# Front of a retention + squared-ReLU kernel: first pair taken before the second, loads and casts reordered, late loads of q in halves

## The chip, the core and the metric

One core of a Trainium2 chip runs the whole program. The metric is the device time of one execution in microseconds (us). A profiled execution gives the trace that all readings come from. Engines: PE (TensorE), DVE (VectorE), ACT (ScalarE), POOL (GpSimd) and SP, whose queue issues most of the DMAs.

## What is computed

```python
for t in range(S):                      # B=4, H=8, S=768, D=64
    state = gamma * state + k[t] outer v[t]
    y[t] = scale * q[t] @ state
x = y.transpose(0, 2, 1, 3).reshape(3072, 512)
out = relu(x @ w_in) ** 2 @ w_out       # w_in 512 x 2048, w_out 2048 x 512
```

All inputs and the output are float32 in HBM. The recurrence over tokens is done in chunks of 128 tokens: inside a chunk by masked scores (q times k, times v), between chunks by a state.

## The kernel before

There are 24 chunks of 128 tokens (6 for each batch) and 11 blocks of tokens for the feed-forward part: the first has four chunks, the others two each. For each chunk the kernel scales q and k by powers of gamma, turns them (PE transposes at first, DMA transposes from chunk 8 on), multiplies scores, masks them on DVE, updates the state in PSUM (`c_ps`), copies it out in bf16 (`s_bd`), forms the outputs (`y`) and copies them as `xt`, the right side of the feed-forward products. The first product of a block is `xt` times `w_in`, copied out by ACT with ReLU (line 859) and squared on DVE (line 830). The second product with `w_out` is done for most blocks by a seven-product scheme: sums of blocks (`s1` to `s4`) are made on DVE and seven instead of eight products are run on PE (`seven_products`, lines 864 to 984, and for half of the first block `last_of_first`, lines 986 to 1109).

The order of work on each engine is written out by hand: instructions stand on their engine in the order in which the Python program makes them, and each waits on semaphores for what it needs. From line 1289 on, `put(place, what)` hangs a step of later chunks on a numbered place between pieces of feed-forward work.

The front, lines 188 to 198 and 1223 to 1285, prepares the first four chunks in two pairs. **Pair 0** is chunks 0 and 1, **pair 2** is chunks 2 and 3. The steps, as the text below names them (m is the pair, g a group of four heads, j the chunk in the pair):

- `scale_q4`, `transpose_q4`: q of the four chunks. `scale_pair_k(m, g)` (line 588) scales k on DVE, or on POOL if told; `transpose_pair_k(m, g)` (lines 613, 614): four transposes on PE, then a copy `kT` on ACT.
- `scores_pair(m, g)` (line 629): 16 small matmuls on quarter tiles of the array, and two masks for DVE (line 637), called `mask_a` and `mask_b`.
- `cast_pair_v(m, r)` (lines 598, 600): v to bf16, on POOL or ACT.
- `state_pair(m, j)` (lines 656, 667, 669): eight matmuls into `c_ps`, then two copies to `s_bd`.
- `outputs_pair(m, g)` (line 680): 16 small matmuls. `finish_pair(m, j)` (lines 696, 708, 710): four matmuls with the state (none for j = 0 of pair 0), then one copy to `xt` on ACT or DVE.
- `first_pair(n)` (line 1128): eight matmuls of the feed-forward part on pair 0 (L850), then ReLU. It needs `xt` of pair 0 and half of the first quarter of `w_in` in bf16. `first_unit(0, 0, c)` (line 1113): 16 matmuls for chunk c of pair 2, c = 2 or 3.
- `cast_w("in", g, halves, on)` (line 348): w_in to bf16 in eight pieces; the letters name the engine of each piece (V DVE, S ACT, G POOL).
- `keep_awake(n)` (line 371): matmuls on zeros between the steps.

After `first_unit(0, 0, 3)` and `state_pair(2, 1)` comes the **dense stage**: 48 matmuls of 512 columns (L850), from 20.32 us on, and then PE work without end until the last block.

The loads of the front go out on SP in this order: q of heads 0 to 3, half of k of pair 0, q of heads 4 to 7, the other half of k of pair 0, k of pair 2, v of pair 0, v of pair 2, then the four quarters of `w_in`, the first two of them in halves. Loads of w_out go out on POOL's queue. `load_q(m, heads)` (line 88) loads q of chunks m and m+1, in as many DMAs as there are parts in `heads`; chunks 6, 8 and 10 have two parts (`heads_of`), chunks 4 and 12 to 22 have one.

Of the kernel before, what the change touches and what calls it, by code (L numbers as in the profile page):

```python
# [14 lines left out]
ALU = mybir.AluOpType  # L15
# [16 lines left out]
def kernel(  # L32
# [9 lines left out]
    nc = tc.nc  # L42
    P = nc.NUM_PARTITIONS

    B, H, S, D = q.shape
# [40 lines left out]
    raw_q, raw_k, raw_v = {}, {}, {}  # L86
# [23 lines left out]
    def load_pair(m, name, src, to, heads=slice(0, H)):  # L110
        b, i = chunks[m]
        if m not in to:
            t = ldpool.tile([P, 2 * H * D], FP32, name=name)
            to[m] = t.rearrange("s (h r d) -> s r h d", h=H, r=2)
        src = src[b, heads, i * C : (i + 2) * C, :].rearrange("h (s r) d -> s h r d", r=2)
        nc.sync.dma_start(to[m].rearrange("s r h d -> s h r d")[:, heads], src)
# [72 lines left out]
    load_pair(0, "kn", k, raw_k, heads_of[0])  # L189
    load_q4(1)  # L190
    load_pair(0, "kn", k, raw_k, heads_of[1])
    load_pair(2, "kn", k, raw_k)
    load_pair(0, "vn", v, raw_v)
    load_pair(2, "vn", v, raw_v)
    load_w_in(0, parts=2)
    load_w_in(1, parts=2)
    for g in range(2, NQ):
        load_w_in(g)
# [180 lines left out]
    def end_awake():  # L379
        idle_ps.clear()  # L380
# [92 lines left out]
    c_ps = [None]  # L473
# [390 lines left out]
    def seven_products(tb):  # L864
# [17 lines left out]
        def add(out, in0, in1, op=ALU.add):  # L882
            nc.vector.tensor_tensor(out=out, in0=in0, in1=in1, op=op)  # L883
# [16 lines left out]
        def rest():  # L900
            first_sums(slice(4, 8))
            pa = (ps_f if tb == 1 else ps_tp).tile([P, HN], FP32, name="psf" if tb == 1 else "tp")
            pb, pe, pd = (ps_f.tile([P, HN], FP32, name="psf") for _ in range(3))
            oa, ob = (opool.tile([P, DM], FP32, name="osb") for _ in range(2))
            a, u, v = (upool.tile([P, HN], FP32, name=f"u{i}") for i in range(3))
            r0 = first[tb] * C
            for js, stop in ((range(0, 6), False), (range(6, 8), True)):
                product(pa[:], a11, b11, js, True, stop)
                product(pe[:], a22, t4, js, True, stop)
                if stop:  # L910
                    nc.scalar.activation(a[:], pa[:], AF.Copy)
                yield
            add(s3, a11, a21, ALU.subtract)
            product(pd[:], s1, t1, range(8), True, True)
            yield
            add(s4, a12, s2, ALU.subtract)
            product(pb[:], s2, t2, range(8), True, True)
            add(u[:], pb[:], a[:])
            yield
            for js in (range(0, 4), range(4, 8)):  # L920
                product(pa[:], a12, b21, js, False, js[-1] == 7)
                if js[0]:
                    nc.scalar.activation(oa[:, 0:HN], pa[:], AF.Copy)  # L923
                yield
            for js in (range(0, 4), range(4, 8)):
                product(pb[:], s3, t3, js, False, js[-1] == 7)
                if js[0]:
                    add(v[:], pb[:], a[:])
                    add(ob[:, HN:DM], pd[:], v[:])
                    add(ob[:, 0:HN], pe[:], v[:])  # L930

                    def last_product():
                        product(pd[:], s4, b22, range(8), False, True)
                        add(oa[:, HN:DM], pd[:], u[:])
                        yield
                        nc.sync.dma_start(out[r0 + C : r0 + 2 * C], ob[:])
                        yield
                        nc.sync.dma_start(out[r0 : r0 + C], oa[:])
                        yield

                    kept.append(last_product())
                yield
# [43 lines left out]
    def last_of_first():  # L986
# [44 lines left out]
        def second_products():  # L1031
            ops = [ps_f.tile([P, DM], FP32, name="psf") for _ in range(2)]
            pa, pe, pd, pb = (
                t[:, n * HN : (n + 1) * HN]
                for t in [ps_f.tile([P, DM], FP32, name="psf") for _ in range(2)]
                for n in range(2)
            )
            oa, ob = (opool.tile([P, DM], FP32, name="osb") for _ in range(2))
            a, u, v = (upool.tile([P, HN], FP32, name=f"u{i}") for i in range(3))
            r0 = 2 * C  # L1040

            def plain(j):
                for f in (2 * j, 2 * j + 1):
                    for c, op in enumerate(ops):
                        nc.tensor.matmul(  # L1045
                            op[:],
                            lhsT=h_of(0, f)[:, 0, c * C : (c + 1) * C],
                            rhs=w_out_bf[f // FPQ][:, f % FPQ, :],
                            start=(f == 0),
                            stop=(f == NFB - 1),  # L1050
                        )
                product(pa, a11, b(0, 0), (j,))

            lo, hi = range(0, 4), range(4, 8)
            for j in range(4):
                plain(j)
                yield
            product(pd, s1, t1, lo)
            product(pb, s2, t2, lo, False)
            yield  # L1060
            for j in range(4, 6):
                plain(j)
                yield
            product(pe, a22, t4, lo, False)
            yield
            plain(6)
            yield
            plain(7)
            nc.scalar.activation(a[:], pa, AF.Copy)

            def store(c):
                osb = opool.tile([P, DM], FP32, name="osb")
                nc.scalar.activation(osb[:], ops[c][:], AF.Copy)
                nc.sync.dma_start(out[c * C : (c + 1) * C], osb[:])

            store(0)
            yield
            product(pd, s1, t1, hi)
            product(pb, s2, t2, hi)
            add(u[:], pb, a[:])  # L1080
            yield
            store(1)
            product(pa, a12, b(1, 0), lo, False)
            yield
            product(pa, a12, b(1, 0), hi, False)
            nc.scalar.activation(oa[:, 0:HN], pa, AF.Copy)
            yield
            product(pb, s3, t3, lo, False)
            yield
            product(pb, s3, t3, hi, False)  # L1090
            add(v[:], pb, a[:])
            add(ob[:, HN:DM], pd, v[:])
            yield
            product(pe, a22, t4, hi)
            add(ob[:, 0:HN], pe, v[:])

            def last_product():
                product(pd, s4, b(1, 1), range(8), False)
                add(oa[:, HN:DM], pd, u[:])
                yield  # L1100
                nc.sync.dma_start(out[r0 + C : r0 + 2 * C], ob[:])
                yield
                nc.sync.dma_start(out[r0 : r0 + C], oa[:])
                yield

            kept.append(last_product())
            yield
# [130 lines left out]
    keep_awake(1)  # L1238
    transpose_pair_k(0, 1, *f)
    mask_a(0)  # L1240
    scale_pair_k(2, 0)
    mask_a(1)
    scale_pair_k(2, 1, nc.gpsimd)
    keep_awake(1)
    transpose_pair_k(2, 0, ps_c, "c_ps")
    mask_b = scores_pair(0, 1, (tp, f), small_pt())
    mask_b(0)
    mask_b(1)
    keep_awake(1)
    cast_pair_v(0, 0)  # L1250
    cast_pair_v(0, 1, on_scalar=True)
    transpose_pair_k(2, 1, *f)
    cast_pair_v(2, 0)
    cast_pair_v(2, 1)
    mask_a = scores_pair(2, 0, (st, f), spare[:, 0:1024])
    keep_awake(1)
    end_awake()
    mask_a(0)
    mask_a(1)
    state_pair(0, 0)  # L1260
    outputs_pair(0, 0, ((ps_y, "y"), f))
    outputs_pair(0, 1)
    mask_b = scores_pair(2, 1, (tp, f), spare[:, 1024:2048])
    mask_b(0)
    cast_w("in", 0, (0,), "GG-V")
    mask_b(1)
    finish_pair(0, 0)
    finish_pair(0, 1)
    cast_w("in", 0, (0,), "--S-")
    state_pair(0, 1, "SV")  # L1270
    outputs_pair(2, 0, ((ps_y, "y"), st))
    first_pair(0)
    cast_w("in", 0, (1,), "GGVV")
    outputs_pair(2, 1)
    finish_pair(2, 0)
    state_pair(2, 0, "VV")
    first_pair(1)
    finish_pair(2, 1, on_scalar=False)
    cast_w("in", 1, (0,), "VVGG")
    first_unit(0, 0, 2)  # L1280
# [10 lines left out]
    parts = {}  # L1291

    def put(place, what, *args):
        parts.setdefault(place, []).append((what, args))
# [66 lines left out]
    for m, d in zip(range(PACK_FROM, NCHUNK), done):  # L1361
        attend2(m, d, done[m - PACK_FROM - 1] if m > PACK_FROM else 0,
                *ahead.get(m, (d - 19, d - 16, d - 13, d - 9)))
        if m >= 12 and m % 2 == 0:
            put(d - 29, load_q, m)
    places = {
        (8, "k"): [26 + j // 2 for j in range(8)],
        (8, "v"): [35 + j // 2 for j in range(8)],
# [52 lines left out]
```

## Time and profile before

| what | us |
|---|---|
| median of 3 runs | 202.81 (202.81 to 202.84) |
| the profiled execution, its own time | 202.86 |
| its span, first to last instruction | 201.1 |
| PE busy in it | 194.7 |
| DVE, ACT, POOL busy | 151.0, 128.0, 81.9 |

The span is what the trace shows; 1.8 us of the execution lie around it. A row of the timeline gives start, duration, engine, source line, operation, tiles, count, and in brackets how long the engine sat idle before it and what ended that. Matmuls of one row are pipelined, so a step's price on PE is read from its start to the start of the next row.

### The profile page before, as it was taken

What the parts mean: (1) busy time and instruction counts of PE and PEld (TensorE: products, weight loads), DVE (VectorE), ACT (ScalarE), POOL (GpSimd) and SP (SyncE); (2) the same over time, 40 slices, a digit from 0 to 9 for tenths busy, and PEclk for the clock granted to TensorE, in tenths of its full rate; (3) what the DMA queues carried; (4) which work ended last, traced back from release to release, by engine and by line L of the source; (5) the groups of instructions that cost most, each with busy time, mean ns of one, the idle gap of its engine ahead of it and who ended that gap; (6) DMA issues with size and microseconds to landing.
All of it is one profiled execution on the core that took longest, in us unless ns stands there. A gap on an engine that the chain in (4) does not pass through costs nothing.

```text
span 201.1 us, 5856 instructions
## 1 busy us (share of the span) xinstructions
PE 194.7 (97%) x2361; PEld 164.6 (82%) x2361; DVE 151.0 (75%) x327; ACT 128.0 (64%) x260; POOL 81.9 (41%) x154
## 2 busy tenths in 40 slices
PE   7799999999999999999999999999999999999992
PEld 2478445779988999899999999999999999999881
DVE  3987899799698896687697697697696696484472
ACT  8885875264853676774766866864865865845710
POOL 8664760899930762154522185116362202200000
PEclk9999999999999999999999999999999999999999
DMA  5999999999988999598998399989899552101102
GB/s 168 355 375 397 345 191 193 231 229 224 313 176 190 169 229 177 165 138 177 186 181 188 115 169 231 210 195 132 148 175 182 173 93 65 71 0 51 56 0 106
DMA packets 92299, 36.03 MB, mean 179 GB/s; under 512 B 68592, under 2 KB 88304, under 8 KB 92272
## 3 DMA queue, kind: packets, MB, share of 16 engines
q1 hardware_dynamic: 73136, 31.47, 65.1%
q0 software_dynamic: 19136, 4.20, 23.0%
q8 instruction: 18, 0.29, 0.6%
q14 instruction: 9, 0.07, 0.1%
HBM read 27.26 MB, written 6.29 MB: 167 GB/s over the span
## 4 chain that ended last, share of the span: by engine, by line
PE 91%; DVE 3%; DMA 2%; ACT 1%; issue 1%; DVEq 0%
PE psf L850 42%; PE psf L887 21%; PE tp L887 7%; PE psf L1045 3%; PE psf L1011 2%; DMA qn<-in_q_dram 2%; PE st L751 2%; PE y L807 2%; PE y L800 2%; PE c_ps L778 2%; PE c_ps L656 1%; PE y L535 1%; PE st L459 1%; DVE qs L562 1%; PE y L371 1%
## 5 line engine op out<-in xcount | busy, mean ns | idle before, releaser
L850 PE MATMUL psf<-xt,w_in_bf 128*128 128x256 bf16 (+2 forms) x864 | 92.3, 261 | 0.0
L850 PEld LDWEIGHTS <-w_in_bf 128*128 128x128 bf16 x864 | 70.7, 98 | 11.2
L859 ACT ACTIVATE h<-psf 128x512 bf16<-128x512 f32 x96 | 56.3, 595 | 23.5 <-PE psf L850 21.2
L729 POOL COPY v_bd<-v 64x512 bf16<-64x512 bf16 x32 | 21.7, 677 | 76.2 <-DVE v L721 75.3
L830 DVE TENSOR_TENSOR h<-h 128x512 bf16<-128x512 bf16 x80 | 33.0, 428 | 18.5 <-ACT h L859 18.1
L887 PEld LDWEIGHTS <-h 128*128 128x128 bf16 x344 | 31.7, 98 | 3.7 <-issue 0.2
L157 POOL DMA_DIRECT2D k_big<-in_k_dram x40 | 26.6, 686 | 0.0
L887 PE MATMUL psf<-w_sum,h 128*128 128x256 bf16 x168 | 23.5, 273 | 0.0
L887 PE MATMUL tp<-w_out_bf,h 128*128 128x256 bf16 x136 | 19.1, 273 | 0.0
L887 PE MATMUL psf<-w_sum,k_bd 128*128 128x256 bf16 x144 | 17.9, 273 | 0.0
L883 DVE TENSOR_TENSOR u<-psf,u 128x256 f32<-128x256 f32 x20 | 8.5, 424 | 12.3 <-PE psf L887 11.4
L883 DVE TENSOR_TENSOR osb<-psf,u 128x256 f32<-128x256 f32 x29 | 11.5, 421 | 6.6 <-PE psf L887 6.3
L887 PEld LDWEIGHTS <-k_bd 128*128 128x128 bf16 x144 | 13.8, 98 | 1.5
L787 ACT ACTIVATE s_bd<-c_ps 64x256 bf16<-64x256 f32 x29 | 10.7, 369 | 6.3 <-PE c_ps L778 6.3
L390 DVE TENSOR_TENSOR qs<-qn,qf 128x512 bf16<-128x512 f32 x20 | 13.7, 690 | 0.0
L788 ACT ACTIVATE s_bd<-c_ps 64x256 bf16<-64x256 f32 x29 | 11.0, 379 | 0.4
L721 DVE TENSOR_TENSOR v<-stage,kf 128x512 bf16<-128x512 f32 x16 | 10.9, 684 | 0.3 <-issue 0.3
L758 DVE TENSOR_TENSOR pt<-st,cmask 128x512 bf16<-128x512 f32 x16 | 11.0, 688 | 0.2
L923 ACT ACTIVATE osb<-tp 128x256 f32<-128x256 f32 x8 | 3.1, 384 | 12.2 <-PE tp L887 12.2
L814 ACT ACTIVATE xt<-y 128x512 bf16<-128x512 f32 x16 | 9.6, 598 | 1.8 <-PE y L807 1.2
L828 ACT ACTIVATE h<-h 128x512 bf16<-128x512 bf16 x16 | 10.1, 629 | 0.5
L883 DVE TENSOR_TENSOR k_bd<-h 128x512 bf16<-128x512 bf16 x18 | 9.9, 552 | 0.3
(148 smaller groups left out, 290.0 us busy)
## 6 DMA issues: line engine op xcount, KB each, us to landing
out_dram<-osb SPq DMA_DIRECT2D x23, 256.0 KB, 2.5
qn<-in_q_dram SPq DMA_DIRECT2D x9, 512.0 KB, 5.4
stage<-in_v_dram SPq DMA_DIRECT2D x32, 96.0 KB, 4.0
stage<-in_moe_w_in_dram SPq DMA_DIRECT2D x4, 512.0 KB, 6.8
stage<-in_moe_w_in_dram SPq DMA_DIRECT2D x2, 1024.0 KB, 10.7
w_out_bf<-in_moe_w_out_dram POOLq DMA_DIRECT2D x4, 512.0 KB, 10.2
kn<-in_k_dram SPq DMA_DIRECT2D x6, 256.0 KB, 5.7
qn<-in_q_dram SPq DMA_DIRECT2D x6, 256.0 KB, 5.8
```

Source lines behind the costliest of these rows:

```text
L157: nc.gpsimd.dma_start(t[rows, 2 * at_w : 2 * (at_w + size), p, hh, :], half_rows(k, b, 2 * p + hh, i + w, size),)
L390: engine.tensor_tensor(out=out, in0=by, in1=table[:, :, None].to_broadcast([P, H, D]), op=ALU.mult)
L721: nc.vector.tensor_tensor(out=v2.rearrange("s (u p) d -> s u p d", u=2), in0=vn, in1=kf2[:, i, :, :, None].to_broadcast([P, 2, NPAIR, D]), ...
L729: nc.gpsimd.tensor_copy(v_bd[rows, :, hh, :], v2[rows])
L758: nc.vector.tensor_tensor(out=pt[:], in0=st[:], in1=cmask2.rearrange("s r t -> s (r t)")[:, None, :].to_broadcast([P, 2 * NPAIR, C // 2]), ...
L787: nc.scalar.activation(s_bd[halves[0], :, 0, :], c[halves[0]], AF.Copy)
L788: nc.scalar.activation(s_bd[halves[1], :, 1, :], c[halves[1]], AF.Copy)
L830: nc.vector.tensor_mul(hv, hv, hv)
L850: nc.tensor.matmul(hp, lhsT=w_in_bf[g][:, cb, fq * 128 : (fq + 1) * 128], rhs=xts[tb][:, cb, cols], start=(cb == 0), stop=(cb == NCB - 1),)
L859: nc.scalar.activation(hv, hp[:], AF.Relu)
L883: nc.vector.tensor_tensor(out=out, in0=in0, in1=in1, op=op)
L887: nc.tensor.matmul(to, lhsT=left[:, j], rhs=right(j) if callable(right) else right[:, j], start=(start and j == 0), stop=(stop and j == NF ...
```

## The change

Four places change.

1. Loads: v of pair 0 goes ahead of k of pair 2, and the first half of w_in's first quarter ahead of v of pair 2.
2. The front's steps: pair 0 is carried through to its outputs before pair 2's k is turned. The casts of w_in's first quarter are spread in another way over POOL, DVE and ACT, the state copies of pair 0 and pair 2 go from DVE to ACT, and the `xt` copy of chunk 0 from ACT to DVE. There is one keep-awake matmul more.
3. In `seven_products` the DVE step that makes `s4` comes one piece later, behind `u`. In `second_products` the copy and store of the second plain output (`store(1)`) come behind the copy of `pa`.
4. `load_q` of chunks 12 to 20 is issued in two halves.

```diff
     load_q4(1)
     load_pair(0, "kn", k, raw_k, heads_of[1])
+    load_pair(0, "vn", v, raw_v)
     load_pair(2, "kn", k, raw_k)
-    load_pair(0, "vn", v, raw_v)
-    load_pair(2, "vn", v, raw_v)
-    load_w_in(0, parts=2)
+    load_w_in(0, parts=2, between=lambda: load_pair(2, "vn", v, raw_v))
     load_w_in(1, parts=2)
...
             product(pd[:], s1, t1, range(8), True, True)
             yield
-            add(s4, a12, s2, ALU.subtract)
             product(pb[:], s2, t2, range(8), True, True)
             add(u[:], pb[:], a[:])
             yield
+            add(s4, a12, s2, ALU.subtract)
...
-            store(1)
             product(pa, a12, b(1, 0), lo, False)
             yield
             product(pa, a12, b(1, 0), hi, False)
             nc.scalar.activation(oa[:, 0:HN], pa, AF.Copy)
+            store(1)
             yield
...
     mask_a(0)
-    scale_pair_k(2, 0)
     mask_a(1)
-    scale_pair_k(2, 1, nc.gpsimd)
-    keep_awake(1)
-    transpose_pair_k(2, 0, ps_c, "c_ps")
+    keep_awake(2)
+    cast_pair_v(0, 0)
+    cast_pair_v(0, 1, on_scalar=True)
     mask_b = scores_pair(0, 1, (tp, f), small_pt())
     mask_b(0)
     mask_b(1)
-    keep_awake(1)
-    cast_pair_v(0, 0)
-    cast_pair_v(0, 1, on_scalar=True)
-    transpose_pair_k(2, 1, *f)
-    cast_pair_v(2, 0)
-    cast_pair_v(2, 1)
-    mask_a = scores_pair(2, 0, (st, f), spare[:, 0:1024])
+    scale_pair_k(2, 1, nc.gpsimd)
+    scale_pair_k(2, 0)
     keep_awake(1)
     end_awake()
-    mask_a(0)
-    mask_a(1)
     state_pair(0, 0)
     outputs_pair(0, 0, ((ps_y, "y"), f))
     outputs_pair(0, 1)
+    finish_pair(0, 0, on_scalar=False)
+    finish_pair(0, 1)
+    transpose_pair_k(2, 0, *f)
+    transpose_pair_k(2, 1, *f)
+    state_pair(0, 1)
+    keep_awake(1)
+    mask_a = scores_pair(2, 0, (st, f), spare[:, 0:1024])
+    end_awake()
+    cast_w("in", 0, (0,), "GGVG")
+    mask_a(0)
+    mask_a(1)
+    first_pair(0)
     mask_b = scores_pair(2, 1, (tp, f), spare[:, 1024:2048])
     mask_b(0)
-    cast_w("in", 0, (0,), "GG-V")
+    cast_pair_v(2, 0)
+    cast_pair_v(2, 1)
+    cast_w("in", 0, (1,), "GGVS")
     mask_b(1)
-    finish_pair(0, 0)
-    finish_pair(0, 1)
-    cast_w("in", 0, (0,), "--S-")
-    state_pair(0, 1, "SV")
+    state_pair(2, 0)
     outputs_pair(2, 0, ((ps_y, "y"), st))
-    first_pair(0)
-    cast_w("in", 0, (1,), "GGVV")
+    first_pair(1)
     outputs_pair(2, 1)
     finish_pair(2, 0)
-    state_pair(2, 0, "VV")
-    first_pair(1)
     finish_pair(2, 1, on_scalar=False)
     cast_w("in", 1, (0,), "VVGG")
     first_unit(0, 0, 2)
...
         if m >= 12 and m % 2 == 0:
-            put(d - 29, load_q, m)
+            put(d - 29, load_q, m, heads_of if m < 22 else (slice(0, H),))
```

## Prediction

> **What bounds the kernel now.** I read the page first, then the busy time by stretches, then the engines' timelines of the first 21 us.
>
> ```profile
> span 201.1 us, 5856 instructions
> PE 194.7 (97%) x2361; PEld 164.6 (82%) x2361; DVE 151.0 (75%) x327; ACT 128.0 (64%) x260; POOL 81.9 (41%) x154
> 100.00:140.00 40.00, 40.00 (x500) 36.38 (x499) 30.24 (x63) 27.03 (x58) 14.47 (x22) 1.00 1.00 179
> ```
>
> PE is busy for 97% of the span, and in the stretch from 100 to 140 us for 40.00 of 40.00, at a granted clock of 1.00. So this kernel is PE's queue of matmuls from end to end: an edit pays only if PE waits less, and it costs what PE waits more. After the start of the dense stage I find two places worth a tenth or more where PE waits (below). All else is the front: when does the dense stage start? Here is PE before that.
>
> ```profile
> 10.46 0.39 PE L371 MATMUL y<-h 128*128 128x512 bf16 x1
> 10.68 0.39 PE L613 MATMUL psf<-ident,k_big 128*128 128x128 bf16 x4
> 11.01 0.24 PE L629 MATMUL st<-qT,kT 64*64 64x128 bf16 x2
> ...
> 11.36 0.39 PE L371 MATMUL y<-h 128*128 128x512 bf16 x1
> 11.68 0.62 PE L656 MATMUL c_ps<-v_bd,k_big 64*128 64x128 bf16 x8
> 12.23 0.24 PE L680 MATMUL y<-pt,v_bd 64*64 64x128 bf16 x1
> ...
> 12.70 0.22 PE L629 MATMUL tp<-qT,kT 64*64 64x128 bf16 x1
> ...
> 13.16 0.40 PE L696 MATMUL psf<-qT,s_bd 128*128 128x128 bf16 x4
> 13.49 0.62 PE L656 MATMUL c_ps<-v_bd,k_big 64*128 64x128 bf16 x8
> ...
> 14.38 1.05 PE L850 MATMUL psf<-xt,w_in_bf 128*128 128x256 bf16 x8
> 15.36 0.24 PE L680 MATMUL y<-h,v_bd 64*64 64x128 bf16 x1
> ...
> 15.71 0.40 PE L696 MATMUL y<-qT,s_bd 128*128 128x128 bf16 x4
> ...
> 17.61 0.40 PE L696 MATMUL st<-qT,s_bd 128*128 128x128 bf16 x4
> 17.84 2.00 PE L850 MATMUL psf<-xt,w_in_bf 128*128 128x128 bf16 x32
> 19.77 0.62 PE L656 MATMUL c_ps<-v_bd,k_big 64*128 64x128 bf16 x8
> 20.32 10.53 PE L850 MATMUL psf<-xt,w_in_bf 128*128 128x512 bf16 x48
> ```
>
> From start to start these rows give the prices: a keep-awake 0.22 (10.46 to 10.68), or 0.32 when other tile shapes follow (11.36 to 11.68); four transposes 0.33; scores 0.35 (11.01 to 11.36); a state 0.55; the outputs of two groups 0.47, of one group 0.35 (15.36 to 15.71); a finish 0.33 (13.16 to 13.49), or some 0.22 before matmuls of its own shape (17.61 to 17.84; transposes alike); a `first_pair` 0.98; both `first_unit` 1.93. There is hardly a gap: the dense stage starts at 20.32 because that much work lies in front.
>
> **The change, part by part.**
>
> *The front.* Up to the keep-awake at 10.46 both programs have the same chain (q, k of pair 0, scores), except that before turns four k tiles of pair 2 at 9.78, in a time in which PE waited anyway. After must do these behind 10.46: +0.22. Summed with the prices above, in the new order, and with no wait at all: keep-awake 0.32, state 0.55, outputs (0,0) 0.24 and (0,1) 0.35, finish 0.22, transposes 0.22 and 0.33, state 0.55, keep-awake 0.32, scores 0.35, `first_pair` 0.98, scores 0.35, state 0.55, outputs 0.35, `first_pair` 0.98, outputs 0.35, two finishes 0.44, units 1.93, state 0.55: 9.93, so the dense stage could start at 20.39. Nothing is saved on PE; the reorder can only add waits. For those I need the other engines.
>
> ```profile
> 10.56 0.69 DVE L637 TENSOR_TENSOR pt<-tp,maskp 128x512 bf16<-128x512 f32 x1 [0.23 <-PE psf L629]
> 11.17 0.68 DVE L637 TENSOR_TENSOR pt<-psf,maskp 128x512 bf16<-128x512 f32 x1
> ```
> ```profile
> 9.43 0.60 ACT L614 ACTIVATE kT<-psf 128x512 bf16<-128x512 bf16 x1 [0.23 <-PE psf L613]
> 10.84 0.63 ACT L598 ACTIVATE v_bd<-vn 128x512 bf16<-128x512 f32 x1
> 12.33 0.77 ACT L667 ACTIVATE s_bd<-c_ps 64x256 bf16<-64x256 f32 x2 [0.38 <-PE c_ps L656]
> 16.14 0.60 ACT L708 ACTIVATE xt<-y 128x512 bf16<-128x512 f32 x1
> ```
> ```profile
> 7.68 2.94 POOL L588 TENSOR_TENSOR k_big<-kn,kfp 128x512 bf16<-128x512 f32 x2 [1.51 <-DMA kn<-in_k_dram]
> 10.57 0.61 POOL L600 CAST v_bd<-vn 128x512 bf16<-128x512 f32 x1
> 12.04 1.18 POOL L600 CAST v_bd<-vn 128x512 bf16<-128x512 f32 x2 [0.86 <-DMA vn<-in_v_dram]
> 13.46 0.82 POOL L358 CAST w_in_bf<-stage 128x256 bf16<-128x256 f32 x2 [0.24 <-DMA stage<-in_moe_w_in_dram]
> 14.81 0.75 POOL L358 CAST w_in_bf<-stage 128x256 bf16<-128x256 f32 x2 [0.53 <-DMA stage<-in_moe_w_in_dram]
> ```
>
> The loads swap slots of one size (512 KB each), so I let each slot keep its landing: v of pair 0 takes the fifth slot, in by about 9.1 (estimate: one slot, some 1.5 us by 10.57 to 12.04, ahead of the sixth), k of pair 2 the sixth, 10.5, w_in's first half 12.0, v of pair 2 13.4, the second half 14.8. Then, step by step:
>
> - v of pair 0 is cast by 9.7 on POOL and, behind `kT` (9.43 + 0.60), by 10.6 on ACT. State (0,0) starts at 10.78, outputs (0,0) at 11.33, (0,1) at 11.57. But (0,1) needs `mask_b(1)`, and that ends as before, at 11.17 + 0.68 = 11.85, since scores (0,1) still hang on the same `kT`. **First wait: 0.34**, to 11.91.
> - Finish (0,1) needs `s_bd`: state ends 11.40, ACT's pair takes 0.77, 12.2. k of pair 2 is ready on DVE at 12.46 (behind the masks) and on POOL near 12.1. Small waits, 0.08 in all. Transposes at 12.52 and 12.74, state (0,1) 13.07, keep-awake 13.62, scores (2,0) 13.94 (ACT's `kT` 13.8), `first_pair(0)` 14.29. Its w_in pieces are cast by 13.3, its `xt` by 13.3: no wait. Scores (2,1) 15.27, state (2,0) 15.62 (v cast by 14.7), outputs (2,0) 16.17, `first_pair(1)` 16.52 (DVE's piece is cast at 16.60 and asked for at 16.74: close), outputs (2,1) 17.50.
> - Finish (2,0) starts at 17.85, finish (2,1) at 18.07, and PE is through at 18.29. The next thing in its queue is `first_unit(0, 0, 2)`, which reads `xt` of (2,0). Before, that copy had time: finish at 15.71, copy 16.14 to 16.74, unit at 17.84, with a state, a `first_pair` and the other finish between. Now only 0.22 us of PE work lies between. The copy starts 0.43 after the finish and takes 0.60, and PE follows some 0.06 later (`s_bd` ends 13.10, PE 13.16): 18.95. **Second wait: 0.66.** The copy of (2,1) on DVE, begun near 18.5, lies beside the first unit.
>
> Dense stage: 20.39 + 0.34 + 0.08 + 0.66 = 21.47, with rounding 21.4 to 21.5: **+1.1 us**. Behind it everything has more time than before: w_in's later quarters land at the old times, and all casts, masks and stores move along. The cover of this sum is that PE is full; no later idle time gives it back.
>
> *`store(1)` and `s4`.* Both stand where PE waits now:
>
> ```profile
> 44.53 1.31 PE L1011 MATMUL psf<-w_sum,h 128*128 128x256 bf16 x8
> ...
> 61.09 1.05 PE L887 MATMUL psf<-w_out_bf,h 128*128 128x256 bf16 x8
> 62.16 0.60 PE L887 MATMUL psf<-w_sum,h 128*128 128x256 bf16 x4
> ```
> ```profile
> 44.32 0.60 ACT L1073 ACTIVATE osb<-psf 128x512 f32<-128x512 f32 x1
> 44.82 0.38 ACT L1086 ACTIVATE osb<-psf 128x256 f32<-128x256 f32 x1
> ```
> ```profile
> 61.09 0.69 DVE L883 TENSOR_TENSOR h<-h,h 128x1024 bf16<-128x1024 bf16 x1
> 61.69 0.42 DVE L883 TENSOR_TENSOR u<-psf,u 128x256 f32<-128x256 f32 x1
> ...
> 108.73 0.43 DVE L883 TENSOR_TENSOR u<-psf,u 128x256 f32<-128x256 f32 x1 [1.12 <-PE psf L887]
> ```
>
> Eight matmuls take 1.31 at 44.53 and 1.05 at 61.09: 0.26 of wait, for the copy of `pa` that ends at 45.20 behind `store(1)`. With the copy first it ends near 44.7 and the wait goes; the next scores then wait some 0.08 for their mask. I take −0.2 (bounds 0 and −0.28). At 62.16 four matmuls stand behind `u`, which stood behind `s4` (61.09): eight matmuls of 0.109 from 61.09 would let them start at 61.96, so −0.18 (bounds 0 and −0.20). In the later blocks DVE idles 1.12 us before `v` (108.73), and `s4`, 0.69, fits there: nothing.
>
> *q in halves.* Five more issues on SP. The list of waits has one line for q:
>
> ```profile
> DVE qs L562 <- DMA qn<-in_q_dram: 1.8, 1, 1.8
> ```
> ```profile
> 57.83 1.17 SPq L94 DMA_DIRECT2D qn<-in_q_dram  x2
> ```
>
> That is the first load of all; no later q was waited for, so an earlier q gains nothing. A half takes SP 0.6 to issue (57.83, two in 1.17), which can push back what stands behind it: stores, loads of v and the DMA transposes of k. I take 0, since no turned k is named in that list either; bounds 0 and +0.6.
>
> *Two rules of the skill.* The Trainium skill, "TensorEngine Tiling (Array Packing)", Key Properties, says that a change of the tiling mode drains the engine. The trace agrees: 0.10 between a keep-awake before its own shape and before another. By that rule alone the order matters for its number of changes, and I count 15 behind 10.46 in the new order against 14: +0.1, which the prices hold already. The Trainium skill, "DMA: Bandwidth & Descriptors", Anatomy of one DMA, (SWDGE path), gives each DMA a fixed 2.0 us, which speaks against halving loads; by it five more would be 10 us of DMA latency, beside PE's work as long as no q is waited for. It is stated for GpSimd's path, and no row here parts latency from transfer.
>
> **The sum**: +1.1 − 0.2 − 0.18 = +0.7. On the profiled execution's 202.86 (span 201.1 and 1.8 around it; 0.05 over the median of 202.81) that is 203.5 us.
>
> **The rivals.**
>
> - *Not slower: the two waits don't come.* Place: the mask at 11.85 and the `xt` copy at 18.3. If both results lay ready when PE asks, only the floor of 20.39 is left, +0.07, and the regained 0.38 wins: 202.86 − 0.31 = 202.55. It decides from where the waits sum to under 0.3. For it: the floor is as low as now. Against: both waits are distances between two instructions that the order fixes, priced by rows. If half of them comes, it is 203.1, no difference. Chance 0.24 for this side: 0.07 faster, 0.17 the same.
> - *The other engines' queues are later than I place them.* DVE's cast for `first_pair(1)` has 0.14 of room, ACT's `kT` for scores (2,0) 0.14, and POOL has one more cast ahead of v of pair 2; POOL's k takes 1.3 to 1.6 (2.94 for two). Half a us late in that row of copies is PE waiting: dense stage near 22, 204.1. Chance 0.15.
> - *The regained waits don't come, or q in halves pushes a turned k behind its scores*: 203.9. Chance 0.08.
> - My forecast, 203.5 give or take 0.3: 0.53.
>
> **Range and chances.** 202.8 to 204.2 leaves out the fast end of the first rival and the far end of the second. 0.2%, 0.4 us, is about what a measurement of this kernel can tell from no change: faster 0.07, same 0.17, slower 0.76.
>
> **What would show it.** In the changed kernel's PE timeline: outputs (0,1) broken off near 11.6 and going on near 11.9; an idle time of about 0.66 ahead of the 32 matmuls of L849, ended by ACT's `xt` copy; the 48 matmuls starting near 21.4; eight matmuls in 1.05 where 1.31 stood; no gap at the u of the second block. I am wrong if the 48 matmuls start before 20.7, or if PE gaps show after them that are not there now.

## The result and the profile after

| what | before | after |
|---|---|---|
| median, us (14 runs each, taken together) | 202.82 (202.80 to 203.11) | 203.28 (203.17 to 203.84) |
| span of the profiled execution | 201.09 | 201.52 |
| landing of the last output | 199.44 | 200.60 |

The ratio of the medians is 1.0022, with a 95% interval of [1.0014, 1.003]: 0.46 us slower, where 0.7 was forecast. The page of after is as full of PE as that of before:

```profile
span 201.5 us, 5862 instructions
PE 195.3 (97%) x2359; PEld 165.0 (82%) x2362; DVE 150.5 (75%) x324; ACT 128.5 (64%) x262; POOL 82.0 (41%) x155
```

So I read PE's timeline, and for each matmul how much later it starts than the same matmul before. First the front (after's lines are one below those of before).

```profile
10.75 0.62 PE L655 MATMUL c_ps<-v_bd,k_big 64*128 64x128 bf16 x8
11.30 0.24 PE L679 MATMUL y<-pt,v_bd 64*64 64x128 bf16 x1
...
11.55 0.22 PE L679 MATMUL psf<-pt,v_bd 64*64 64x128 bf16 x1
11.88 0.21 PE L679 MATMUL y<-pt,v_bd 64*64 64x128 bf16 x1
...
12.24 0.40 PE L695 MATMUL psf<-qT,s_bd 128*128 128x128 bf16 x4
12.48 0.62 PE L612 MATMUL psf<-ident,k_big 128*128 128x128 bf16 x8
...
18.03 0.39 PE L695 MATMUL st<-qT,s_bd 128*128 128x128 bf16 x4
18.88 1.95 PE L849 MATMUL psf<-xt,w_in_bf 128*128 128x128 bf16 x32 [0.46 <-ACT xt L707]
20.76 0.62 PE L655 MATMUL c_ps<-v_bd,k_big 64*128 64x128 bf16 x8
21.31 10.53 PE L849 MATMUL psf<-xt,w_in_bf 128*128 128x512 bf16 x47
```

The dense stage starts at 21.31, 0.99 later than the 20.32 of before. Two waits make it: 11.55 to 11.88 (0.33, of which 0.05 is the pace of these matmuls: 0.28), and 18.03 to 18.88 (0.85, of which the finish itself is 0.22: 0.63). The row of the units names ACT's `xt` copy. What is left, 21.31 − 0.28 − 0.63 = 20.40, is the floor of 20.39 (the prediction's sum without any wait), so next to nothing of the small waits came. The two results came when the prediction had them, the second mask (begun at 11.14) at 11.82 and the copy at 18.83; DVE's and ACT's timelines:

```profile
11.14 0.68 DVE L636 TENSOR_TENSOR pt<-psf,maskp 128x512 bf16<-128x512 f32 x1
```
```profile
18.23 0.60 ACT L707 ACTIVATE xt<-y 128x512 bf16<-128x512 f32 x1
```

Behind the front, the transposes of q in PE's timeline of before, then PE's timeline of after:

```profile
46.80 0.61 PE L420 MATMUL tp<-ident,qs 128*128 128x128 bf16 x8
```
```profile
45.52 1.04 PE L1010 MATMUL psf<-w_sum,h 128*128 128x256 bf16 x8
...
47.59 0.90 PE L419 MATMUL tp<-ident,qs 128*128 128x128 bf16 x8
...
62.18 1.05 PE L886 MATMUL psf<-w_out_bf,h 128*128 128x256 bf16 x8
63.07 0.60 PE L886 MATMUL psf<-w_sum,h 128*128 128x256 bf16 x4
```

Eight matmuls take 1.04 where 1.31 stood, and from the eight to the four behind `u` it is 0.89 instead of 1.07: both old waits are gone. But the eight transposes of q, 0.61 before, take 0.90: a new wait of 0.28, ahead of the fifth. Two more waits stand at the four matmuls that update the state in the later blocks (`state2`, L777): 0.10 and 0.14 ahead of the last of the four, at 94.8 and 139.6, and a little ahead of the ones before it. The shift of PE runs: +0.99 (front), −0.28 (45 us), +0.09 (a mask, 46), +0.29 (transposes of q, 48), −0.18 (62), +0.11 and +0.16 (`state2`) = +1.18. Yet the span is only 0.43 longer. So 0.75 came back **behind the last matmul**.

There SP waits for everything that is still under way. Its DMAs go in turn to eight completion semaphores, here called lanes 0 to 7, and at the end SP waits for lane 0, 1, ... 7 in this order, then drains. SP's instructions of that last line, before and after, from the landing of the last output (199.44 and 200.60) on:

```profile
L1416 SPq EVENT_SEMAPHORE  x6: 28/28/28, 199.5 to 200.2; - x6
L1416 SPq DRAIN  x1: 13/13/13, 200.2 to 200.2; - x1
```
```profile
L1415 SPq DRAIN  x2: 7/10/13, 200.7 to 200.8; - x2
L1415 SPq EVENT_SEMAPHORE  x1: 28/28/28, 200.6 to 200.6; - x1
```

In before six waits, the first of them for the last output, follow that landing, in after one. The times of each, from the trace (us), with three of the experiments below; the lanes of the last three outputs are marked `*`:

```
                lane 0   1       2       3       4       5       6       7       drain   last landing
before          198.71*  199.19* 199.46* 199.55  199.62  200.04  200.12  200.18  200.25  199.44
after           199.70   199.78  199.85  199.91  199.97  200.03* 200.37* 200.61* 200.68  200.60
e2_q            198.50   198.58  198.64  198.71  198.77  198.83* 199.18* 199.43* 199.49  199.41
e6_q6           199.43*  199.49  199.56  199.62  199.68  199.74  199.80* 199.86* 199.93  199.41
e9_stores2      198.35   198.42  198.92* 199.40* 199.71* 199.78  199.84  199.90  199.97  199.70
```

A wait for a lane that is long done costs 0.06 to 0.09. Besides, one step takes about 0.41, and in every trace that can show it, it ends at the same place of SP's program, the instruction with number 207 in the trace, counted from zero (`e9_stores2` in its expectation counts it as the 209th): lane 5 in before (199.62 to 200.04), lane 0 in after and in `e2_q`, the wait ahead of lane 0 in `e6_q6` and `e5_stores5`. In `e9_stores2` it is the wait for lane 2, and an output that lands there at 198.90 hides it. In before both, the slow step and the waits for later lanes, came behind the last output, drain 0.81 after its landing. The five extra DMAs of the halved q move the last three outputs from lanes 0 to 2 to lanes 5 to 7, and that instruction ahead of the landing: drain 0.08 after it.

### The profile page after: what moved, and what is told of

The parts are those of the page before. It is cut to its first block, busy times and chain, and to the rows that moved or that the text cites. A ratio compares the mean times of both kernels' runs of the same rounds, so it can differ in the third digit from the quotient of the medians.

```text
span 201.5 us, 5862 instructions
## 1 busy us (share of the span) xinstructions
PE 195.3 (97%) x2359; PEld 165.0 (82%) x2362; DVE 150.5 (75%) x324; ACT 128.5 (64%) x262; POOL 82.0 (41%) x155
## 4 chain that ended last, share of the span: by engine, by line
PE 89%; DVE 4%; DMA 3%; issue 1%; SPq 1%; POOL 1%; ACT 1%; POOLq 0%; DVEq 0%
PE psf L849 42%; PE psf L886 21%; PE tp L886 7%; PE psf L1044 3%; DMA kn<-in_k_dram 3%; PE psf L1010 2%; PE st L750 2%; PE y L806 2%; PE c_ps L777 2%; PE y L799 2%; PE y L534 1%; PE c_ps L655 1%; DVE qs L389 1%; PE st L458 1%; DVE osb L882 1%
```

## The experiments

All are compared with runs of the kernel before on the same chip: 202.87 beside `e1_front`, `e2_q`, `e3_stalls` and `e4_best`, 202.86 beside the others. The first number of each result is the median (6 to 13 runs), round brackets hold the lowest and the highest, square brackets the 95% interval of the ratio to before.

**Theory.** The front costs +1.0 by its two waits; `store(1)` and `s4` gain less than their old waits because new ones come; the halved q gains 0.73 by the number of its DMAs alone. **Rivals**: halved q gains by landing earlier; the 0.73 is chance; the new waits come only from PE being earlier.

**`e1_front`**, the loads and the front alone (parts 1 and 2 of the change).

> Only the front of the change (order of the loads, order of the first 21 us); q whole, store(1) and s4 as before. Theory (front costs what the trace of after shows, and the tail is ruled by the number of SyncE's DMAs): the dense stage starts at 21.3 as in after, the waits of 0.28 and 0.18 at 45 and 62 us stay, the last drain of SyncE stands 0.8 us behind the last landing as in before: 203.8 us (203.6 to 204.0), so slower than after. Rival (the front is cheaper than 1.0 because something later gives it back): 203.3 or less, and the last matmul less than 0.7 later than in before.

203.95 (203.88 to 204.01), ratio 1.0045 [1.0029, 1.0061], +1.08. PE's timeline has the same wait:

```profile
18.01 0.39 PE L695 MATMUL st<-qT,s_bd 128*128 128x128 bf16 x4
18.86 1.95 PE L849 MATMUL psf<-xt,w_in_bf 128*128 128x128 bf16 x32 [0.46 <-ACT xt L707]
20.74 0.62 PE L655 MATMUL c_ps<-v_bd,k_big 64*128 64x128 bf16 x8
21.29 1.04 PE L849 MATMUL psf<-xt,w_in_bf 128*128 128x512 bf16 x3
```

The last landing is at 200.5, the drain 0.8 behind it. Nothing later gives the front's microsecond back; the rival falls. On the contrary, a tenth is added: PE is 0.96 later than before behind the front and 1.06 from the transposes of q on, which take 0.71 here (47.76) instead of 0.61.

**`e2_q`**, the halved loads alone.

```diff
-            put(d - 29, load_q, m)
+            put(d - 29, load_q, m, heads_of if m < 22 else (slice(0, H),))
```

> Only the halved loads of q. Theory (five more DMAs on SyncE's eight lanes move the last three outputs from the first lanes to the last, and the final waits in lane order are through when the last output lands): the last matmul ends as in before, the drain stands 0.1 instead of 0.8 us behind the last landing, 202.1 us (202.0 to 202.3). Rival A (halves do nothing, as the prediction priced them): 202.8. Rival B (halves land earlier and take waits from PE): the last matmul ends earlier than in before.

202.11 (202.09 to 202.15), ratio 0.9954 [0.994, 0.9969]. PE's matmuls start when they did before, within 0.06 in the front and within 0.01 from the dense stage on, so rival B falls, and the drain (table) is 0.76 earlier. The forecast priced this edit at nothing.

**`e5_stores5`**, five more DMAs that are not q: in blocks 5 to 9 one of the two stores is cut in two.

```diff
-                        nc.sync.dma_start(out[r0 + C : r0 + 2 * C], ob[:])
+                        for cols in (slice(0, HN), slice(HN, DM)) if tb >= 5 else (slice(0, DM),):
+                            nc.sync.dma_start(out[r0 + C : r0 + 2 * C, cols], ob[:, cols])
```

> The kernel before with q whole, but five of its stores of the output (the first of the two of blocks 5 to 9) cut in two halves of columns: five more DMAs on SyncE that have nothing to do with q. Theory (what counts is the number of DMAs, modulo the eight lanes): last three outputs on lanes 5, 6, 7 as with the halved q, drain 0.1 behind the last landing, 202.1 us (202.0 to 202.3). Rival (the halved q itself, its landing or its order on the queue, gives the gain): 202.8.

202.08, ratio 0.9962 [0.9951, 0.9974]: the whole gain, with q whole.

**`e6_q6`**, `heads_of` for chunk 22 too, six more DMAs.

> The kernel before with the q of chunk 22 in halves as well: six more DMAs instead of five. Theory (lanes): the last output falls on lane 0, which is waited for first, so seven waits of 0.06 to 0.07 us follow its landing, without the step of 0.41: drain 0.5 to 0.6 behind the last landing, 202.6 us (202.5 to 202.7), slower than with five halves although more q is halved. Rival (halves help as such): 202.1 or less.

202.55, ratio 0.998 [0.9971, 0.9989]. Eight waits follow the landing at 199.41:

```profile
L1416 SPq EVENT_SEMAPHORE  x8: 28/28/28, 199.4 to 199.9; - x8
L1416 SPq DRAIN  x1: 13/13/13, 199.9 to 199.9; - x1
```

**`e9_stores2`**, the same edit as `e5_stores5` with `tb >= 8`, two more DMAs.

> The kernel before with two stores of the output cut in two (blocks 8 and 9): two more DMAs. Theory (lanes, and a step of 0.41 us at one fixed instruction of SyncE, its 209th, which here is the wait for lane 2 and so ahead of the last landing): the last output falls on lane 4, three waits of 0.065 follow it, drain 0.25 to 0.3 behind the last landing, 202.3 us (202.2 to 202.4). Rival (lanes alone, no fixed step: each lane 0.73 / 5 = 0.15): 202.5 to 202.6. Rival (number of DMAs does not matter): 202.8.

202.38, ratio 0.9971 [0.9956, 0.9986]. Four waits follow the landing at 199.70, the first for that landing itself:

```profile
L1417 SPq EVENT_SEMAPHORE  x4: 28/28/28, 199.7 to 199.9; - x4
L1417 SPq DRAIN  x1: 13/13/13, 200.0 to 200.0; - x1
```

The order of the four times, 202.1 for five, 202.4 for two, 202.55 for six, 202.86 for none, is that of the theory; neither the amount of halved q nor "more DMAs" gives it. What the 0.41 at this instruction is, no run shows; that it stays at that instruction while all around it moves, they do.

**`e3_stalls`**, `store(1)` and `s4` alone (part 3).

> Only store(1) behind the copy of pa, and s4 behind u. Theory: the two PE waits of 0.28 and 0.18 go, the tail stays as in before: 202.4 us (202.3 to 202.5), if no wait takes their place. Rival (what is gained at 45 us is given back at the transposes of q near 47, as in after): 202.6, with a PE idle time of 0.2 to 0.3 ended by DVE's qs.

202.74, ratio 0.9987 [0.9976, 0.9999]. Neither was right: the two old waits go, no wait comes at 47, and still only 0.13 is left. The rest is lost later. PE's timeline around the second block, and at 93 us:

```profile
60.87 1.05 PE L887 MATMUL psf<-w_out_bf,h 128*128 128x256 bf16 x8
61.76 0.60 PE L887 MATMUL psf<-w_sum,h 128*128 128x256 bf16 x4
```
```profile
93.28 0.44 PE L778 MATMUL c_ps<-v,k_big 128*128 128x64 bf16 x4
93.56 0.71 PE L850 MATMUL psf<-xt,w_in_bf 128*128 128x256 bf16 x5
```

PE is 0.40 earlier than before at 62 us, but at 93 us the four matmuls of `state2` take 0.28 from start to start, instead of the 0.11 of `e7_s4once` below, and at 138 us there is another such wait: PE's lead over before is 0.40, then 0.24, then 0.12. DVE's timeline shows why:

```profile
91.33 0.42 DVE L883 TENSOR_TENSOR u<-psf,u 128x256 f32<-128x256 f32 x1 [0.74 <-PE psf L887]
91.68 0.68 DVE L883 TENSOR_TENSOR v_bd<-h,k_bd 128x1024 bf16<-128x1024 bf16 x1
92.27 0.68 DVE L721 TENSOR_TENSOR v<-stage,kf 128x512 bf16<-128x512 f32 x1
```

The row with `v_bd<-h,k_bd` is `s4`. It now follows `u` and stands ahead of the scaling of v (L721), which ends at 92.95. PE's queue waits for that v, and then takes four waits one after another (at 93.00, 93.12, 93.25, 93.42 in the trace), so the fourth weight load starts only at 93.50.

**`e4_best`**, parts 3 and 4 on the front of before.

> The front of before, with halved q, store(1) and s4 moved. Theory: the sum of the two single edits, 201.7 to 201.9 us, faster than before and after. Rival A (halves do nothing): 202.4. Rival B (the single edits get into each other's way at 45 to 48 us): 202.0 or more.

202.02, ratio 0.9961 [0.9948, 0.9973]: `e2_q` less 0.09, where part 3 alone gave 0.13 (`e3_stalls`). That is the time of rival B, but not its place: in the trace PE's lead shrinks at 93 and 138 us, as in `e3_stalls`, and not at 45 to 48.

**`e7_s4once`**, the same with `s4` moved in the block of 62 us alone.

```diff
+            if tb > 1:
+                add(s4, a12, s2, ALU.subtract)
             product(pb[:], s2, t2, range(8), True, True)
             add(u[:], pb[:], a[:])
             yield
-            add(s4, a12, s2, ALU.subtract)
+            if tb == 1:
+                add(s4, a12, s2, ALU.subtract)
```

> The front of before, halved q, store(1) moved, and s4 behind u in the block of 62 us alone, ahead of the products as before in all later blocks. Theory (s4 behind u makes the scaled v late at 93 and 138 us, and state2 waits there 0.12 to 0.14): these two waits go, the gains at 45 and 62 us stay, 201.75 us (201.6 to 201.85), below the 202.02 with s4 moved in every block. Rival (the waits at 93 and 138 us come from being 0.4 us earlier, whatever stands where on VectorE): 202.0.

201.75 (201.69 to 202.97), ratio 0.9948 [0.9931, 0.9966], the fastest kernel of this study. DVE's timeline has `s4` in the idle time ahead of `u` again, v ends at 92.86, and PE does not wait although it is nearly as early as in `e3_stalls` (0.34 ahead of before, where that was 0.40):

```profile
90.57 0.69 DVE L883 TENSOR_TENSOR v_bd<-h,k_bd 128x1024 bf16<-128x1024 bf16 x1
91.39 0.42 DVE L883 TENSOR_TENSOR u<-psf,u 128x256 f32<-128x256 f32 x1
92.17 0.69 DVE L721 TENSOR_TENSOR v<-stage,kf 128x512 bf16<-128x512 f32 x1 [0.35 <-issue]
```
```profile
93.34 0.28 PE L778 MATMUL c_ps<-v,k_big 128*128 128x64 bf16 x4
93.45 0.82 PE L850 MATMUL psf<-xt,w_in_bf 128*128 128x256 bf16 x6
```

**`e10_cast`**: after, with POOL's cast of v of chunk 6 behind the two memsets that followed it. It asks for the wait at 48 us, which neither `e3_stalls` nor `e4_best` has. In after DVE's two scalings of q take 1.69, in before 1.28 (the first row); POOL's row of after is the cast that was running when the second began (46.95):

```profile
45.34 1.28 DVE L390 TENSOR_TENSOR qs<-qn,qf 128x512 bf16<-128x512 f32 x2
```
```profile
46.35 1.69 DVE L389 TENSOR_TENSOR qs<-qn,qf 128x512 bf16<-128x512 f32 x2
```
```profile
46.73 0.76 POOL L405 CAST v_bd<-vn 128x512 bf16<-128x512 f32 x1
47.44 0.94 POOL L1380 MEMSET k_big<- 64x1024 bf16 x1
```

```diff
-        nc.gpsimd.tensor_copy(
-            v_bd[:, :, ::3, :], vn.rearrange("s (p hh) d -> s p hh d", hh=2)
-        )
+        if m != 6:
+            cast_v(m)
...
+    def cast_v(m):
+        vn = raw_v.pop(m).rearrange("s (p hh) d -> s p hh d", hh=2)
+        nc.gpsimd.tensor_copy(v_bds[m % 2][:, :, ::3, :], vn)
...
+    put(34, cast_v, 6)
```

> After, with GpSimd's cast of v of chunk 6 moved behind the two memsets that followed it. Theory (VectorE's second scaling of q at 46.95 takes 1.09 instead of 0.68 us because it begins while that cast is running; in before it began ahead of the cast and took 0.69): it takes 0.7, the wait of 0.28 ahead of the transposes of q at 48.1 goes, 203.0 us (202.9 to 203.1). Rival (the scaling is stretched by something else, a DMA or a fixed place in its instructions; or a memset does the same as a cast): 203.3.

203.03, ratio to before 1.0008 [0.999, 1.0026], 0.25 below after's median. The traced execution took 203.35: the second load of q landed at 7.08 instead of 6.72, and the front starts 0.36 later. In its DVE and POOL timelines the scalings take 1.28, beside a memset:

```profile
46.69 1.28 DVE L389 TENSOR_TENSOR qs<-qn,qf 128x512 bf16<-128x512 f32 x2
```
```profile
47.00 1.50 POOL L1383 MEMSET k_big<- 64x1024 bf16 x2
48.36 0.70 POOL L409 CAST v_bd<-vn 128x512 bf16<-128x512 f32 x1
```

The transposes of q take 0.61 again (PE, 47.94). The Trainium skill, "SBUF — State Buffer", Who interferes with whom, says that a VectorE instruction with two SBUF inputs contends with a GpSimd instruction that reads SBUF, not with one that only writes it, and that the order of issue decides which of two is held off. These rows agree: +0.41 beside the cast, nothing beside the memset. The other rows of the traces bear it out. From 21 us on, in all thirteen, 134 steps of DVE with two inputs in SBUF began while a cast or copy of POOL had more than 0.3 us to run, and 132 of them took longer than their kind; of 80 that began beside a memset, none did. The time added is some 0.15 less than what POOL had left: in before 0.41 for 0.56 (101.11), 0.29 for 0.44 (71.64), 0.20 for 0.35 (85.92).

It is not all of the wait at 48 us. `w_sum` at 44.40 in after (1.09, and 0.68 in `e10_cast`) stood beside no cast, only beside POOL's DMA issues. In the traces of `e8_cover` and `e11_all`, below, PE waits at the transposes of q as well (0.28 and 0.15), though both scalings take their usual 0.68 in the one and the cast is out of the way in the other: there a step of DVE beside such issues is longer (0.83 for 0.42 at 45.33, 0.96 for 0.68 at 46.46). Why these are, no run shows.

**`e8_cover`**: after, with `state_pair(2, 1)` ahead of `first_unit(0, 0, 2)`.

> After, with the eight small matmuls of state (2,1) put ahead of the first unit that waits for the xt copy of (2,0), instead of behind both units. Theory (the second wait of the front, 0.57, is the distance from the finish through ScalarE's copy to the unit, and other work of PE covers it): the wait shrinks to 0.1 or less, the dense stage starts at 20.8 instead of 21.3, 202.75 us (202.65 to 202.9). Rival (the later stages wait for something else that sets the time, the front only hides it): 203.2 or more.

202.45, ratio 0.9974 [0.9957, 0.9991]: 0.83 below after, where 0.53 was expected. **`e11_all`** joins this, the cast and `s4` in one block.

> After with all three: state (2,1) ahead of the unit, the cast of chunk 6 behind the memsets, and s4 behind u in the block of 62 us alone. Theory (the terms add): 203.28 - 0.55 - 0.28 - 0.25 = 202.2 us (202.1 to 202.4), so faster than before, but slower than the 201.75 of the same edits on the front of before, by the first wait of 0.27 and the floor of 0.07 and what is left of the second. Rival (terms get into each other's way): 202.5 or more.

202.47, ratio 0.997 [0.9953, 0.9988]; its fastest run is 202.18. PE's timeline shows the cover at work, with no wait between the finish and the units:

```profile
18.78 0.39 PE L696 MATMUL st<-qT,s_bd 128*128 128x128 bf16 x4
19.10 0.62 PE L656 MATMUL c_ps<-v_bd,k_big 64*128 64x128 bf16 x8
19.65 12.32 PE L850 MATMUL psf<-xt,w_in_bf 128*128 128x128 bf16 x79
```

From the finish to the state it is 0.32, and the units follow directly: the second wait (0.57 in the expectation, which counts the finish at 0.28) is a distance that other work covers. The sums are not shown. The runs of these two kernels are spread over 1.4 and 0.8 us. Both were traced in their slowest execution (203.64 and 202.99), in which the second load of q lands at 7.46 and 7.47 instead of 6.72, so all of the front starts 0.75 later. Less these 0.75 the traced `e11_all` comes to 202.24, near the sum of 202.2 and its fastest run, but its median is 0.23 above that; `e8_cover` comes to 202.9, so its trace does not show the execution that its median stands for. Why `e8_cover` gains 0.3 more than its wait, and `e11_all` nothing beyond it, stays open.

## Why the prediction came out as it did

The time lay in the range and the sign was right; the sum was 0.24 too high. That it came so near is luck in part: PE ended 1.18 later, where 0.7 was forecast, and a gain of 0.75 that the forecast did not have stood against it. Without that gain the time would have been 204.03, inside the range still, but not in 203.5 give or take 0.3.

- *The front, +1.1*: right, in place, cause and size. +0.99 in the trace; +1.08 alone (`e1_front`), of which 0.10 is lost only at the transposes of q. First wait 0.28 for 0.34, small waits next to nothing for 0.08, second 0.63 for 0.66, floor as summed. `e8_cover` and `e11_all` show that the second hangs on the order of two steps.
- *`store(1)`, −0.2*: right alone (`e3_stalls`: −0.29 at 45 us, +0.07 at the mask). On the new front it was lost again: 0.29 at the transposes of q, of which the front alone makes 0.10. So the single edits do not add: `e1_front`, `e2_q` and `e3_stalls` sum to +0.19, and after is +0.46. The prediction asked what is late next and named the mask; it did not look at DVE's scaling of q, 0.34 ahead of its use before, nor at what runs on POOL beside it.
- *`s4`, −0.18; "in the later blocks ... nothing"*: the gain came (−0.18), the "nothing" failed. The row quoted (108.73) is a `u`, and its 1.12 of idle time lies behind the scaling of v; where `s4` now goes, between the `u` before it and v, DVE does not idle (before's rows of `s4`, `u` and v stand below the list). So v comes later in such blocks, and in two of them PE waits for it: +0.11 and +0.16 in after. `e7_s4once` shows it.
- *q in halves, "I take 0; bounds 0 and +0.6"*: the step that failed most. The mechanism weighed (a q that lands earlier, a queue that is pushed back) does give nothing, as `e2_q` shows in PE's timeline. But five more DMAs change the lanes of the last outputs and the place of one slow instruction of SP: −0.75. I priced the queue of SP, but not what stands at its end; the end of the span went into the sum as a constant.
- *"Wrong if PE gaps show after them that are not there now"*: they did, at 48, 94.8 and 139.6 us, +0.56 in all. *Rivals*: neither the first (waits that don't come) nor the second (queues half a us late) happened; the regained wait at 45 was lost as in the third, but through DVE's scaling of q, not through a turned k.

```profile
105.64 0.69 DVE L883 TENSOR_TENSOR v_bd<-h,k_bd 128x1024 bf16<-128x1024 bf16 x1
106.58 0.42 DVE L883 TENSOR_TENSOR u<-psf,u 128x256 f32<-128x256 f32 x1 [0.26 <-PE psf L887]
106.92 0.68 DVE L721 TENSOR_TENSOR v<-stage,kf 128x512 bf16<-128x512 f32 x1
```

## What to carry to other kernels

An edit that changes how many DMAs a queue issues can change the end of the program, even if no one waits for those DMAs: read what stands between the last landing and the last instruction, and count. Where a step is moved "into idle time", ask in each block what stands behind it on that engine and how long ahead of its use that is ready; an average idle time does not say so. A copy placed directly between two steps of the bound engine is a wait, whose length is the distance of the two rows, and moving an independent step between them takes it away.

## What was not expected of the hardware

- Waits of SP for lanes that are long done take 0.06 to 0.09 us each, in fixed order; where the last output lands decides how many follow it (0.08 to 0.81 us from the last landing to the drain).
- One instruction of SP, number 207 of its trace in every kernel here that can show it, takes about 0.41 us, whatever it waits for.
- Four semaphore waits of PE's queue ahead of four weight loads took about 0.12 us each, one after another: with v ready 0.48 us ahead of the first matmul PE did not wait (`e7_s4once`, 92.86 to 93.34), with 0.33 it did (`e3_stalls`, 92.95 to 93.28).
- DVE's scaling of q took 0.68 us beside a memset of POOL and 1.09 beside a cast; steps of DVE with two inputs in SBUF are held up by what a cast or copy of POOL has left to run, less some 0.15 us.
